# Decode attention with a parallel MLP: two weight rows to a partition, K0 loaded first, some w2 rows on the ACT queue, b1 spread by DVE

## Chip, cores, metric

One core of a Trainium2 chip. The time is the device time of one execution in microseconds (us), lower is better. The *span* is the stretch that the trace covers, from the first instruction to the last; the time is some 2 us longer. That remainder, time minus span, is called "outside the span" here. The runs record spans to 0.1 us, so a single value of it is good to 0.05 us.

Engines: PE is the matmul engine (PEld its weight loads), DVE, ACT and POOL are the vector, scalar and GpSimd engines, and SP issues most loads. The granted clock is the share of PE's full clock that the throttle allowed.

## The reference, cut to what matters

```python
x = A_x                                   # [2, 1, 576]
xn = layernorm(x)
# A: attention of one new token over the last 2048 cached positions (16 KV heads, 32 query heads, 128 wide)
q = xn @ wq                               # wq [576, 4096]
o = softmax(q @ K^T * 128**-0.5) @ V      # K and V are the bulk of the traffic
a = o @ wo                                # wo [4096, 576]
# B: MLP with squared ReLU
h = relu(xn @ w1 + b1) ** 2               # w1 [576, 4608]
b = h @ w2 + b2                           # w2 [4608, 576]
return x + a + b
```

Everything is bf16. K and V together are 33.6 MB of the 53.6 MB that have to be read once; the weights are the other 20 MB.

## The kernel before

It streams K and V in eight units of 2 MB each, and the weights between them. Nearly all loads are issued by SP. In names, K0 is K of the first unit; w2x and w2y are 240 and 16 rows of w2 that are loaded apart, in four loads and one, and `mlp_x` does their matmuls; "the remainder" is the last 64 of the 576 rows of wq or w1.

```python
NFULL = D // P                      # 4 full blocks of 128 rows, and a remainder of 64 rows
const = ctx.enter_context(tc.tile_pool(name="const", bufs=1))      # allocated first
kvpool = ctx.enter_context(tc.tile_pool(name="kvpool", bufs=6))    # K, V and w2 buffers, behind it
wbig = ctx.enter_context(tc.tile_pool(name="wbig", bufs=NFULL))
# ...
def issue_w(tiles, wt, c, name, width, lrem):          # wq and w1: one load per 128 rows
    if c < NFULL:
        tl = wbig.tile([P, WBW], BF16, tag="wbig", name=f"{name}_{c}")
        nc.sync.dma_start(out=tl[:, 0:width], in_=wt[c * P:(c + 1) * P, :])
# ...
def issue_w2x():                                       # 240 rows of w2, five partitions at a time
    ...
    nc.sync.dma_start(out=w2x_sb[i:XP:XP // XE, :], in_=rows[i])
# ...
x_sb = const.tile([B, D], BF16, name="x_sb")
nc.scalar.dma_start(out=x_sb[:], in_=x2d)
eps_t = const.tile([B, 1], F32, name="eps_t")
warm = const.tile([B, 2], F32, name="warm")            # 32 bytes to a partition as allocated
# ...
k0 = issue_kv(k_tiles, A_k_cache, 0, "k", parts=2)
issue_wq(0)
k0[0]()
issue_wq(1)
k0[1]()
for c in range(2, KC):
    issue_wq(c)
# ...
sel4 = const.tile([NG4, P], BF16, name="sel4")         # spreads b1 over the groups of the MLP
nc.gpsimd.memset(sel4[:], 0.0)
for b in range(B):
    nc.gpsimd.tensor_copy(out=sel4[:, b:P:32], in_=ident[0:NG4, 0:NG4])
# ...
mlp_h_end()
mlp_x()                                                # the matmuls of w2x and w2y
step(NU - 1, {}, with_pv=False)                        # transposes and scores of the last K
# ...
for i in range(len(W2P)):                              # w2, the last rows in pieces of 4, 2 and 1
    mlp_o(*W2P[i], last=(i == len(W2P) - 1))
nc.vector.tensor_copy(out=fin_sb[:], in_=out_ps[:])
nc.sync.dma_start(out=out2d[:, 0:OH], in_=fin_sb[0:B, :])
nc.scalar.dma_start(out=out2d[:, OH:D], in_=fin_sb[32:32 + B, :])
```

## Time and profile before

| | before |
|---|---|
| time, median of 3 runs | 137.41 us (137.2 to 137.5) |
| span of the profiled run | 135.0 us |
| first load packet starts, last load lands | 1.76 us, 131.27 us |
| output landed | 133.45 us |
| busiest engine, PE | 98.1 us, 73% |

The first lines of the page:

```profile
span 135.0 us, 4131 instructions
PE 98.1 (73%) x1876; PEld 79.8 (59%) x1876; DVE 56.8 (42%) x134; ACT 44.7 (33%) x51; POOL 10.2 (8%) x34
```

### The profile page before, as it was taken

The page shows a single profiled execution, that of the slowest core. Times are in us where ns is not written, and L with a number is a line of the kernel's source. Part 1 is how long each engine was busy: PE and PEld are TensorE (multiplying, and loading weights), DVE is VectorE, ACT ScalarE, POOL GpSimd, SP SyncE. Part 2 cuts the span into 40 slices and gives each one's busy share as a digit, 9 for nine tenths or more (in the row PEclk, how much of TensorE's full clock was granted, in tenths as well). Part 3 has the DMA queues.
Part 4 walks back from the last instruction along what each step waited for, and adds up shares of the span by engine and source line. Part 5 has one row for each costly group of instructions (what it writes and reads, how often), then busy time and mean ns, then how long its engine had stood idle before and what let it go on. Part 6 is the DMA issues. An engine that isn't in the chain of part 4 may idle for free.

```text
span 135.0 us, 4131 instructions
## 1 busy us (share of the span) xinstructions
PE 98.1 (73%) x1876; PEld 79.8 (59%) x1876; DVE 56.8 (42%) x134; ACT 44.7 (33%) x51; POOL 10.2 (8%) x34
## 2 busy tenths in 40 slices
PE   1039946699969179719997998796565999669961
PEld 0018616598859079607986997784115599655530
DVE  7532405574564634640455655644224024650001
ACT  6703504465254127110834625421021055010000
POOL 8300000110110110110001001001100000110000
PEclk9999995559999559955996899996555558965899
DMA  4999999999999999999999999999999999999950
GB/s 120 423 428 425 427 430 442 408 447 403 451 385 437 431 417 433 398 409 438 422 432 417 432 413 428 395 428 415 414 441 427 427 413 420 431 407 417 404 228 1
DMA packets 5492, 53.87 MB, mean 399 GB/s; under 512 B 694, under 2 KB 844, under 8 KB 1360
## 3 DMA queue, kind: packets, MB, share of 16 engines
q1 hardware_dynamic: 5404, 53.61, 95.1%
q8 instruction: 14, 0.23, 0.7%
q0 software_dynamic: 64, 0.01, 0.0%
q14 instruction: 2, 0.02, 0.0%
q10 hardware_dynamic: 8, 0.00, 0.0%
HBM read 53.62 MB, written 0.00 MB: 397 GB/s over the span
## 4 chain that ended last, share of the span: by engine, by line
DMA 87%; PE 6%; SPq 2%; DVE 1%; ACT 1%; issue 1%; ACTq 0%
DMA k<-in_A_k_cache_dram 39%; DMA w_rem<-in_B_w_dram 20%; DMA w<-in_B_w_dram 16%; DMA wq<-in_A_wq_dram 11%; PE out_ps L236 3%; PE kT_ps L271 2%; SPq L115 1%; SPq L109 1%; DVE hrow L376 1%; PE hb_ps L385 1%; ACT t L375 1%; PE ha_ps L382 1%; PE h_ps L366 0%; DVE fin_sb L502 0%; DVE hT_sb L391 0%
## 5 line engine op out<-in xcount | busy, mean ns | idle before, releaser
L271 PE MATMUL kT_ps<-ident,k 128*128 128x128 bf16 x512 | 44.9, 251 | 6.4 <-DMA k<-in_A_k_cache_dram 6.1
L274 ACT COPY kT<-kT_ps 128x1024 bf16<-128x1024 bf16 x32 | 32.1, 1011 | 36.0 <-PE kT_ps L271 34.4
L271 PEld LDWEIGHTS <-k 128*128 128x128 bf16 x512 | 37.2, 114 | 8.3 <-DMA k<-in_A_k_cache_dram 6.4
L276 DVE COPY kT<-kT_ps 128x1024 bf16<-128x1024 bf16 x32 | 21.8, 687 | 26.4 <-PE kT_ps L271 25.8
L286 PE MATMUL sc_ps<-qT_all,kT 128*128 128x8 bf16 x512 | 21.6, 168 | 4.5 <-ACT kT L274 2.6
L286 PEld LDWEIGHTS <-kT 128*128 128x128 bf16 x512 | 18.8, 99 | 6.3 <-ACT kT L274 3.5
L323 PE MATMUL oT_ps<-pT,v 128*128 128x8 bf16 x512 | 15.9, 166 | 2.0 <-ACT pT L303 1.5
L323 PEld LDWEIGHTS <-v 128*128 128x128 bf16 x512 | 14.4, 96 | 3.5 <-issue 3.4
L303 ACT ACTIVATE pT<-sub 128x512 bf16<-128x512 f32 x8 | 5.1, 631 | 26.0 <-DVE sub L300 26.0
L305 DVE TENSOR_REDUCE l<-pT 128x8 f32<-128x512 bf16 x8 | 8.5, 1065 | 5.3 <-ACT pT L303 5.3
L236 PE MATMUL out_ps<-wo,ws 128*2 128x288 bf16 x64 | 7.2, 403 | 3.5 <-DVE ws L345 3.5
L296 POOL PARTITION_ALL_REDUCE gmax<-m x8 | 2.9, 366 | 84.7 <-DVE m L294 84.7
L236 PEld LDWEIGHTS <-hT_sb 128*2 128x2 bf16 (+2 forms) x94 | 4.7, 96 | 5.4 <-issue 2.2
L292 DVE TENSOR_REDUCE m<-sc_ps 128x8 f32<-128x512 f32 x8 | 5.5, 692 | 4.7 <-PE sc_ps L286 4.6
L236 PEld LDWEIGHTS <-ws 128*2 128x2 bf16 x64 | 3.4, 110 | 6.0 <-DVE ws L345 3.6
L236 PE MATMUL out_ps<-w,hT_sb 128*2 128x288 bf16 x68 | 5.4, 302 | 1.4 <-DMA w<-in_B_w_dram 1.3
L366 PE MATMUL h_ps<-w,xnT 128*2 128x384 bf16 x48 | 4.3, 514 | 1.8 <-DMA w<-in_B_w_dram 1.7
L300 DVE TENSOR_TENSOR sub<-sc_ps,gm 128x512 f32<-128x512 f32 x8 | 5.5, 689 | 0.2
L307 POOL PARTITION_ALL_REDUCE lsum<-l x8 | 3.2, 400 | 23.7 <-DVE l L305 23.7
L502 DVE CAST fin_sb<-out_ps 34x288 bf16<-34x288 f32 x1 | 0.5, 451 | 10.3 <-PE out_ps L236 10.3
L366 PEld LDWEIGHTS <-xnT 128*2 128x2 bf16 x60 | 1.8, 104 | 5.1 <-issue 5.1
L236 PE MATMUL out_ps<-b_sb,ones_b 1*2 1x288 bf16 x2 | 0.4, 394 | 5.1 <-DMA b_sb<-in_B_b_dram 5.1
(73 smaller groups left out, 48.2 us busy)
## 6 DMA issues: line engine op xcount, KB each, us to landing
v<-in_A_v_cache_dram SPq DMA_DIRECT2D x8, 2048.0 KB, 23.8
k<-in_A_k_cache_dram SPq DMA_DIRECT2D x7, 2048.0 KB, 26.7
wo<-in_A_wo_dram SPq DMA_DIRECT2D x4, 1152.0 KB, 23.2
w<-in_B_w_dram SPq DMA_DIRECT2D x4, 1152.0 KB, 30.6
wq<-in_A_wq_dram SPq DMA_DIRECT2D x4, 1024.0 KB, 13.7
w<-in_B_w_dram SPq DMA_DIRECT2D x3, 1296.0 KB, 27.8
k<-in_A_k_cache_dram SPq DMA_DIRECT2D x2, 1024.0 KB, 7.4
w_rem<-in_B_w_dram SPq DMA_DIRECT2D x1, 576.0 KB
```

What stands on the lines that cost most here:

```text
L236: nc.tensor.matmul(out_ps[32 * i:32 * i + B, :], lhsT=lhsT, rhs=rhs_of(i * OH, (i + 1) * OH), start=start, stop=stop, skip_group_check=True)
L271: nc.tensor.transpose(out=kT_ps[:, i * P:(i + 1) * P], in_=k_sb[:, j * Dh:(j + 1) * Dh], identity=ident[:])
L274: nc.scalar.copy(out=kT[:], in_=kT_ps[:])
L276: nc.vector.tensor_copy(out=kT[:], in_=kT_ps[:])
L286: nc.tensor.matmul(sc_ps[:, g * JG + i, :], lhsT=kT[:, i * P:(i + 1) * P], rhs=qT_all[:, b, tq * NC:(tq + 1) * NC], start=True, stop=True)
L292: nc.vector.tensor_reduce(out=m1[:], in_=sc_ps[:].rearrange("p j c -> p c j"), axis=AX.X, op=ALU.max)
L300: nc.vector.tensor_tensor(out=sub[:], in0=sc_ps[:], in1=gm2[:].unsqueeze(1).to_broadcast([P, NJ, NC]), op=ALU.subtract)
L303: nc.scalar.activation(out=pT[:], in_=sub[:], func=ACT.Exp, scale=scale)
L305: nc.vector.tensor_reduce(out=l1[:], in_=pT[:].rearrange("p j c -> p c j"), axis=AX.X, op=ALU.add)
L307: nc.gpsimd.partition_all_reduce(lsum[:], l1[:], channels=P, reduce_op=ReduceOp.add)
L323: nc.tensor.matmul(oT_ps[:], lhsT=v_sb[:, j * Dh:(j + 1) * Dh], rhs=pT_tiles[u][:, j, :], start=(j == 0), stop=(j == NJ - 1))
L366: nc.tensor.matmul(mlp["ps"][k][32 * g:32 * g + B, :], lhsT=xnT[:, xc, :], rhs=rhs, start=False, stop=(c == KC - 1), skip_group_check=True ...
```

## The change

Its intent: fewer and longer pieces for wq and w1, a simpler start, a small load off the SP queue, and three small operations off POOL. The diff, cut to its core (index and naming lines left out):

```diff
-    wbig = ctx.enter_context(tc.tile_pool(name="wbig", bufs=NFULL))
+    RW = 2
+    wbig = ctx.enter_context(tc.tile_pool(name="wbig", bufs=NFULL // RW))
 ...
-            tl = wbig.tile([P, WBW], BF16, tag="wbig", name=f"{name}_{c}")
-            nc.sync.dma_start(out=tl[:, 0:width], in_=wt[c * P:(c + 1) * P, :])
+            tl = wbig.tile([P, RW * WBW], BF16, tag="wbig", name=f"{name}_{i}")
+            rows = wt[0:NFULL * P, :].rearrange("(p r) n -> p (r n)", r=NFULL)
+            nc.sync.dma_start(out=tl[:, 0:RW * width], in_=rows[:, i * RW * width:(i + 1) * RW * width])
+            for r in range(RW):
+                tiles[i * RW + r] = tl[:, r * width:(r + 1) * width]
 ...
+            if r0 == 0:      # the three last pieces of w2 share one tile
+                w2_last.append(wbig.tile([P, nr * D], BF16, tag="wbig", name=f"w2_{g}"))
+            tl = w2_last[0][:, r0 * D:r1 * D]
 ...
-            nc.sync.dma_start(out=w2x_sb[i:XP:XP // XE, :], in_=rows[i])
+            tc.keep_in_program_order(nc.scalar.dma_start(out=w2x_sb[i:XP:XP // XE, :], in_=rows[i]))
 ... (w2y likewise)
-    k0 = issue_kv(k_tiles, A_k_cache, 0, "k", parts=2)
-    issue_wq(0); k0[0](); issue_wq(1); k0[1](); then wq 2, 3 and the remainder
+    for f in issue_kv(k_tiles, A_k_cache, 0, "k"):
+        f()
+    for i in range(NFULL // RW + 1):
+        issue_wq(i)
 ... (x is transposed in the columns c, c+4, c+8, ... to match; K0 is transposed before all of q)
-    nc.gpsimd.memset(sel4[:], 0.0)
-    for b in range(B):
-        nc.gpsimd.tensor_copy(out=sel4[:, b:P:32], in_=ident[0:NG4, 0:NG4])
+    nc.vector.tensor_copy(out=sel4[:].rearrange("p (g s) -> p g s", s=32),
+                          in_=ident[0:NG4, 0:NG4].unsqueeze(2).to_broadcast([NG4, NG4, 32]))
 ...
     mlp_h_end()
-    mlp_x()
     step(NU - 1, {}, with_pv=False)
     ...
     wo_acc(NQ - 2)
+    mlp_x()
```

More of the change, by code (lines that the diff above doesn't have):

```diff
@@ L110, in issue_kv, with issue_w @@
                 for i in range(parts)]
-    def issue_w(tiles, wt, c, name, width, lrem):
-        if c < NFULL:
-            tl = wbig.tile([P, WBW], BF16, tag="wbig", name=f"{name}_{c}")
-            nc.sync.dma_start(out=tl[:, 0:width], in_=wt[c * P:(c + 1) * P, :])
+    def issue_w(tiles, wt, i, name, width, lrem):
+        if i < NFULL // RW:
+            tl = wbig.tile([P, RW * WBW], BF16, tag="wbig", name=f"{name}_{i}")
[3 more added lines that the diff above has]
+                tiles[i * RW + r] = tl[:, r * width:(r + 1) * width]
         else:
@@ L118, in issue_w @@
             nc.sync.dma_start(out=tl[:, 0:lrem], in_=wt[NFULL * P:D, :].rearrange("r (s l) -> (r s) l", s=S))
-        tiles[c] = tl
+            tiles[NFULL] = tl
     def issue_wq(c):
@@ L138, in issue_wo @@
         wo_tiles[tq] = tl
+    w2_last = []
     def issue_w2(g, r0, r1):
         nr = FR if g < NG4 - 1 else FT
-        pool, tag = (kvpool, "kv") if g < NG4 - 1 else (wbig, "wbig")
-        tl = pool.tile([P, (r1 - r0) * D], BF16, tag=tag, name=f"w2_{g}_{r0}")
+        if g < NG4 - 1:
+            tl = kvpool.tile([P, nr * D], BF16, tag="kv", name=f"w2_{g}")[:]
+        else:
+            if r0 == 0:
+                w2_last.append(wbig.tile([P, nr * D], BF16, tag="wbig", name=f"w2_{g}"))
+            tl = w2_last[0][:, r0 * D:r1 * D]
         rows = B_w2[g * HW:g * HW + nr * P, :].rearrange("(p r) n -> p (r n)", r=nr)
-        nc.sync.dma_start(out=tl[:], in_=rows[:, r0 * D:r1 * D])
+        nc.sync.dma_start(out=tl, in_=rows[:, r0 * D:r1 * D])
         w2_tiles[(g, r0)] = tl
@@ L155, in issue_w2x @@
             rows = B_w2[FX0:FX0 + XR * XP, :].rearrange("(e i r) n -> i e (r n)", e=XE, r=XR)
-            nc.sync.dma_start(out=w2x_sb[i:XP:XP // XE, :], in_=rows[i])
+            tc.keep_in_program_order(nc.scalar.dma_start(out=w2x_sb[i:XP:XP // XE, :], in_=rows[i]))
             if not x_parts:
-                nc.sync.dma_start(out=w2y_sb[:], in_=B_w2[FX0 + XR * XP:F, :])
+                tc.keep_in_program_order(nc.scalar.dma_start(out=w2y_sb[:], in_=B_w2[FX0 + XR * XP:F, :]))
     x_sb = const.tile([B, D], BF16, name="x_sb")
@@ L165 @@
     nc.scalar.activation(out=warm[:, 0:1], in_=eps_t[:], func=ACT.Sqrt)
-    k0 = issue_kv(k_tiles, A_k_cache, 0, "k", parts=2)
-    issue_wq(0)
-    k0[0]()
-    issue_wq(1)
-    k0[1]()
-    for c in range(2, KC):
-        issue_wq(c)
+    for f in issue_kv(k_tiles, A_k_cache, 0, "k"):
+        f()
+    NW = NFULL // RW + 1
+    for i in range(NW):
+        issue_wq(i)
     ones_f = const.tile([P, P], F32, name="ones_f")
@@ L208 @@
     for c in range(NFULL):
-        nc.tensor.transpose(out=pro_ps[:, c, :], in_=xn_sb[:, c * P:(c + 1) * P], identity=ident[:B, :B])
+        nc.tensor.transpose(out=pro_ps[:, c, :], in_=xn_sb[:, c:NFULL * P:NFULL], identity=ident[:B, :B])
     for sg in range(S):
@@ L436, in step @@
         softmax(u)
-    for g in range(4):
+    for g in range(NG):
         transposes(0, g)
-    q_block(0)
-    q_block(1)
-    for g in range(4, NG):
-        transposes(0, g)
-    for c in range(2, KC):
+    for c in range(KC):
         q_block(c)
@@ L470 @@
         if u == 4:
-            for c in range(KC):
-                issue_w1(c)
+            for i in range(NW):
+                issue_w1(i)
         if u + 3 < NU:
```

## The prediction

> **What bounds the kernel now.** I looked first at the slices of the page, to see which resource has no holes.
>
> ```profile
> DMA  4999999999999999999999999999999999999950
> GB/s 120 423 428 425 427 430 442 408 447 403 451 385 437 431 417 433 398 409 438 422 432 417 432 413 428 395 428 415 414 441 427 427 413 420 431 407 417 404 228 1
> DMA packets 5492, 53.87 MB, mean 399 GB/s; under 512 B 694, under 2 KB 844, under 8 KB 1360
> ```
>
> The DMA row stands at 9 from the second slice to the thirty-eighth, while the busiest engine, PE, is at 73% of the span. A 9 only means "at least 90%", so I asked for the busy time of each engine in stretches of the span, to see how full the engines are (columns: stretch, its length, busy us of PE, PEld, DVE, ACT, POOL, granted clock, DMA share, GB/s).
>
> ```profile
> 25.00:45.00 20.00, 16.76 (x384) 15.94 (x384) 11.62 (x24) 9.04 (x10) 1.84 (x5) 0.84 1.00 422
> 65.00:85.00 20.00, 18.02 (x429) 16.67 (x426) 11.82 (x25) 10.16 (x11) 1.53 (x4) 0.91 1.00 422
> 120.00:131.40 11.40, 9.34 (x121) 5.64 (x119) 0.84 (x4) 0.00 (x0) 0.32 (x1) 0.73 0.90 366
> ```
>
> The DMA share is 1.00 at 422 GB/s, and not even 18 us of PE work in 20 us lowers it. In the packet records the first load packet starts at 1.76 us and the last one lands at 131.27 us. These 129.5 us of stream, 1.76 us before it and 3.7 us after it make the span of 135.0 us; the measured time is 137.2 to 137.5, some 2.3 us more than the span.
>
> Next, the chain that ended last, to see whether anything else sets the end.
>
> ```profile
> DMA 87%; PE 6%; SPq 2%; DVE 1%; ACT 1%; issue 1%; ACTq 0%
> ...
> 109.30 22.09 DMA w<-in_B_w_dram
> 131.38 0.04 issue
> 131.42 0.68 PE out_ps L236 x6
> 132.10 0.02 issue
> 132.12 0.45 DVE fin_sb L502
> ```
>
> It is DMA but for the short calculations between, and it closes with the last w2 rows, six matmuls, one copy and the output. PE at the end says the same:
>
> ```profile
> 125.30 2.83 PE L236 MATMUL out_ps<-w,hT_sb 128*2 128x288 bf16 x36
> 129.24 1.27 PE L236 MATMUL out_ps<-w,hT_sb 128*2 128x288 bf16 x18 [1.12 <-DMA w<-in_B_w_dram]
> 130.66 1.42 PE L236 MATMUL out_ps<-w,hT_sb 128*2 128x288 bf16 x14 [0.16 <-DMA w<-in_B_w_dram]
> ```
>
> PE stood idle 1.12 us for the third w2 load and again for the pieces after it: it is ahead of the stream when the stream ends.
>
> Last, how the loads are issued, since the change moves five of them to ACT.
>
> ```profile
> 4.81 0.55 SPq L109 DMA_DIRECT2D k<-in_A_k_cache_dram  x1
> 5.53 0.54 SPq L109 DMA_DIRECT2D v<-in_A_v_cache_dram  x1
> 8.65 0.54 SPq L109 DMA_DIRECT2D k<-in_A_k_cache_dram  x1
> 10.96 0.54 SPq L109 DMA_DIRECT2D v<-in_A_v_cache_dram  x1
> 13.44 0.85 SPq L156 DMA_DIRECT2D w2x_sb<-in_B_w_dram  x1
> ...
> v<-in_A_v_cache_dram SPq DMA_DIRECT2D x8, 2048.0 KB, 23.8
> k<-in_A_k_cache_dram SPq DMA_DIRECT2D x7, 2048.0 KB, 26.7
> ```
>
> From 8.65 us on the issues come 2.4 us apart, the time of one 1 MB load, so each waits for a landing. The semaphores in the trace tell which: there are eight, handed out in turn to all loads of SP and ACT together (x_sb on ACT has the first, and the eighth load after it, K1, waits for that one). So a load waits for the eighth load before it. The last lines are the time from issue to landing: 23.8 and 26.7 us, of which a 2 MB load's own transfer is about 5 us at 422 GB/s. Some 18 to 22 us of work is therefore queued ahead of each load, and a delay of an issue costs nothing until it exceeds that.
>
> **What the Trainium skill says.** "DMA: Bandwidth & Descriptors", section "Specifications", gives a fabric ceiling of 435 GB/s for the 16 engines; the trace runs at 422, 97% of it, so only about 3% could be won by any shape of transfer. The same page, section "Why small descriptors are slow (HBM only)", has a fixed overhead of about three cycles for each packet. The trace agrees: its records give a median of 309 ns for a packet of 8,192 B and 614 ns for one of 16,384 B, so 2 x 309 - 614 = 4 ns is all that joining two of them saves. Section "Issuing engines are not separate DMA queues" says that starting DMAs from several engines saves only the sequencer's issue time; SP issues 42 loads at about 0.5 us, under 25 us in all, so that is not scarce here. Section "Why a DMA increments its semaphore by 16 and not by 1" says a load of 5 partitions runs on five engines only; each w2x load does have five packets of 13,824 B. The queue doesn't change that.
>
> **The change part by part.**
> Bytes: the same 53.6 MB.
> wq: 512 packets of 8,192 B become 256 of 16,384 B: 256 x 4 ns / 16 engines = 0.06 us. K0 in one load: 128 x 4 / 16 = 0.03 us. w1: 512 packets of 9,216 B (median 351 ns) become 256 of 18,432 B. From the 8,192 and 16,384 B packets the slope is 305 ns per 8,192 B with 4 ns fixed, which gives 690 ns for 18,432 B against 702 for two: 256 x 12 / 16 = 0.19 us. Five loads fewer (two of wq, two of w1, one of K0) save one 9 ns completion packet on each engine: 0.05 us. Together 0.3 us off the stream, all of it on the path.
> First packet: before, the first issue is a wq load of 0.40 us; K0 issues in 0.65 us. If the stream starts by that much later it costs up to 0.25 us; I take 0.1.
> w2x and w2y on ACT: five issues (4 x 0.75 + 0.43 = 3.4 us) leave SP, which spends most of its time waiting, and come to ACT, busy 44.7 of 135 us. Twenty packets of 518 ns on five engines remain 2.1 us on each of these five, whichever queue they come from. Nothing on the path.
> K0 first: q needs the remainder of wq, which lands last of these loads in both orders (19.1 us before), so the scores of unit 0 do not start earlier. PE does the 64 transposes of K0 in one go instead of in two. Nothing.
> b1 spread by DVE: takes a memset of 0.2 us and two copies of 0.19 us from POOL (10.2 us busy) and puts one small DVE copy, about 0.15 us, near the start. Nothing.
> mlp_x later: 26 matmuls, 3.26 us, leave the place before the transposes of the last K (104.4 us) for the tail. PE gains 3.26 us before and loses it after; with over 1.1 us of idle time for w2 and 2.2 us more for softmax between 117 and 121 us, it still waits for the last load. Nothing.
> wbig as two buffers of double width: the last w2 pieces wait for a pair of w1 blocks; both are calculated by 97 us, long before the last issue (114.2 us). Nothing.
> Sum: -0.3 + 0.1 = -0.2 us: 137.4 becomes 137.2.
>
> **Rivals.**
> (a) ACT stands in the ring of eight. An early w2x issue on ACT may have to wait there until a load eight before it lands, 7 to 19 us into the kernel, and behind it stand the LayerNorm square root and half of the K evacuations. For it: the semaphores show one ring for both engines, and ACT runs in order. Against a loss: it delays PE by at most some 10 us near the start, and 18 to 22 us of queued loads keep the stream full; PE needs 98 of 129 us and can catch up. If the buffers did run dry it would be 1 to 5 us: 138.5 to 142.
> (b) A new wait at the end: the three last w2 pieces share one tile now. If their matmuls waited for all three, 14 instead of 6 would follow the last landing: 8 x 0.1 = 0.8 us more, 138.2. Against: K0's halves share a tile before, and its transposes start at 10.58 us, ahead of the second half's landing (12.9 us).
> (c) Five engines end earlier or later. Engines drift apart by up to 3.3 us in mid-stream (completion times of one load), and at the end the 16 end some 1.5 us apart. If the new order evens this out it wins up to 0.7 us: 136.7. If it skews, as much is lost.
> (d) Pieces of 16 KB at a 32 KB pitch (wq) read HBM worse, or rows of 18,432 B better, than I reckon. No run shows it yet; 8.9 MB of 53.6 are concerned (21 us), so 5% either way is 1 us.
>
> **Range and chances.** The sum of certain terms is -0.2 us; (c) and (d) are symmetric at about 0.7 us, (a) and (b) only cost. Hence 136.4 to 138.3. Two per cent is 2.7 us. Faster by that much would need most of the 3% between 422 and 435 GB/s, which packets cannot give: 3%. Slower by that much needs (a) with a dry queue: 6%. The rest, 91%, is within 2%.
>
> **What would show it right or wrong.** DMA share 1.00 and 418 to 426 GB/s in the same stretches, 640 fewer data packets, the last load landing at 131.0 to 131.4 us, the same six matmuls after it. Rival (a) would show as a long ACT gap before 20 us, and only a DMA share under 0.97 somewhere would make it cost. Rival (b) would show 14 matmuls after the last landing. I am wrong if the time lies outside the range, or if the stretch between first and last packet differs from 129.2 us by more than 1 us.

## The result and the profile after

| | before | after |
|---|---|---|
| time, median of 4 runs | 137.45 us (137.20 to 137.64) | 136.46 us (136.43 to 136.55) |
| ratio, 95% interval | | 0.9930 [0.9913, 0.9947] |
| span, median | 135.2 us | 134.65 us |
| time outside the span, median | 2.13 to 2.21 us | 1.84 us |

Ratios here and below are the mean time of one kernel's fast runs over that of the other's of the same rounds, so not quite the ratio of the medians that are quoted. Executions over 1.5% slower than the fastest of the same kernel are left out of the means. The span of before is the median of the 11 runs that accompany each group of experiments. So the change is worth 0.95 to 1 us, within 2%: some 0.55 us of it in the span and 0.35 us outside.

The page of the changed kernel, first the engines and the stream:

```profile
span 134.7 us, 4124 instructions
PE 100.8 (75%) x1876; PEld 83.2 (62%) x1876; DVE 56.9 (42%) x135; ACT 44.3 (33%) x51; POOL 9.7 (7%) x31
...
GB/s 152 409 422 434 428 433 419 438 414 439 404 418 439 415 412 433 410 426 429 423 428 419 423 421 422 430 415 423 408 442 428 428 424 407 416 413 424 398 235 1
DMA packets 4772, 53.87 MB, mean 400 GB/s; under 512 B 614, under 2 KB 764, under 8 KB 1280
...
DMA 87%; PE 8%; SPq 2%; issue 0%; DVE 0%; ACT 0%; ACTq 0%
```

There are 720 fewer packets with the same bytes: the 640 data packets of the prediction and 80 completions. DMA is still 87% of the chain. The same stretches as before (stretch, length, busy us of PE, PEld, DVE, ACT, POOL, granted clock, DMA share, GB/s; the share can pass 1.00 because the records of packets overlap, at times 19 at once):

```profile
25.00:45.00 20.00, 17.34 (x344) 17.08 (x344) 9.60 (x19) 9.22 (x11) 1.53 (x4) 0.60 1.01 425
65.00:85.00 20.00, 17.41 (x408) 16.19 (x408) 11.83 (x25) 9.15 (x10) 1.53 (x4) 0.91 1.01 427
120.00:131.40 11.40, 10.34 (x112) 5.48 (x109) 0.00 (x0) 0.00 (x0) 0.00 (x0) 0.72 0.87 356
```

425 and 427 GB/s stand where 422 stood, but this is no general gain: in the other stretches between 8 and 120 us the rates are 428, 418, 424 and 417 where they were 430, 420, 424 and 418. Even a granted clock of 0.60 in the first stretch leaves the DMA share at 1.01. The chain that ended last runs through an ACT issue in its middle, and closes as before:

```profile
40.92 0.06 ACT kT L282
40.97 6.26 DMA w2x_sb<-in_B_w_dram
47.24 0.02 issue
47.25 0.02 SPq L110
47.27 0.03 issue
47.30 24.59 DMA k<-in_A_k_cache_dram
...
109.10 22.13 DMA w<-in_B_w_dram
131.23 0.04 issue
131.27 0.68 PE out_ps L244 x6
131.95 0.02 issue
131.97 0.45 DVE fin_sb L505
```

The last lines come 0.15 us earlier than before (131.27 for 131.42). PE at the end has the w2x matmuls in its tail now, and is still ahead of the stream:

```profile
120.30 3.04 PE L244 MATMUL out_ps<-w2x_sb,hT_sb 20*2 20x288 bf16 x24
...
129.11 2.83 PE L244 MATMUL out_ps<-w,hT_sb 128*2 128x288 bf16 x32 [0.81 <-DMA w<-in_B_w_dram]
```

The last number is the idle time before the group: PE waited 0.81 us for a w2 load. The three microseconds of w2x work in the tail were absorbed, and still six matmuls follow the last landing.

**What the stream itself won.** Packet records of the two traces: the mean busy time of an engine over all load packets fell from 128.35 to 127.72 us, 0.63 us. By size: the w1 pieces took 512 x 354.5 ns and take 256 x 694.5 ns (means, the first over all packets of 9,216 B, half of which are wo's), over 16 engines 0.23 us. The 768 packets of 8,192 B (mean 320.8 ns) gave way to 384 of 16,384 B; with all packets of 16,384 B together (1,920 x 618.6 before, 2,304 x 620.3 after) that is another 0.31 us. Completions and small differences are the other 0.09 us. Against it the first packet starts at 2.13 us instead of 1.76, 0.38 us later. Of this, 0.23 us is K0's longer issue (0.63 us, where wq's took 0.40); the rest has no record. The engines don't end together: the 16 completions of the last w2 load lie between 128.50 and 131.75 us before and between 128.14 and 131.60 after, and the last of them comes 1.00 and 1.17 us after their mean. The three add up, 0.38 - 0.63 + 0.17 = -0.08, about what the trace shows: the stream ends 0.14 us earlier in this pair (131.13 for 131.27).

**What comes after the stream.** The output lands 2.18 us after the last load in both. Then SP goes through the completion semaphores of its loads and stores. The instructions of the kernel's closing line, before and then after (queue and operation, count, ns shortest/median/longest, first and last start in us):

```profile
L530 SPq EVENT_SEMAPHORE  x8: 17/28/28, 132.9 to 134.9; - x8
...
L530 SPq DRAIN  x3: 7/7/13, 134.2 to 134.5; - x3
```

```profile
L533 SPq EVENT_SEMAPHORE  x8: 17/28/28, 132.8 to 134.6; - x8
...
L533 SPq DRAIN  x3: 7/7/13, 133.8 to 134.1; - x3
```

The first DRAIN marks the end of this walk: 0.72 us after the landing of the output before (133.45 to 134.17), 0.53 us after the change (133.30 to 133.83). What follows it is the same 0.84 and 0.83 us. The semaphore records show why. Loads and stores of SP and ACT take eight semaphores in turn, numbers 100, 102 and 113 to 118. Six waits of SP at the end go through 113 to 118 in this order, about 62 ns from one to the next. Before, there are 43 loads, and the two stores get 114 and 115: SP stands at them until the stores have landed, and 116, 117 and 118 come on top, 3 x 62 ns = 0.19 us. With 38 loads the stores get 117 and 118, and the other waits are over by then.

**Outside the span**, the runs (not the trace) show 0.35 us less. Which part of the change does it is a matter for the experiments.

### The profile page after: what moved, and what is told of

Read it like the earlier page. It is cut to its first block, busy times and chain, and to the rows that moved or that the text cites. A ratio compares the mean times of both kernels' runs of the same rounds, so it can differ in the third digit from the quotient of the medians.

```text
span 134.7 us, 4124 instructions
## 1 busy us (share of the span) xinstructions
PE 100.8 (75%) x1876; PEld 83.2 (62%) x1876; DVE 56.9 (42%) x135; ACT 44.3 (33%) x51; POOL 9.7 (7%) x31
## 4 chain that ended last, share of the span: by engine, by line
DMA 87%; PE 8%; SPq 2%; issue 0%; DVE 0%; ACT 0%; ACTq 0%
DMA v<-in_A_v_cache_dram 47%; DMA k<-in_A_k_cache_dram 18%; DMA w<-in_B_w_dram 16%; PE kT_ps L279 5%; DMA w2x_sb<-in_B_w_dram 5%; PE oT_ps L331 1%; PE sc_ps L294 1%; SPq L110 1%; SPq L117 1%; PE out_ps L244 1%; SPq L122 0%; DVE fin_sb L505 0%; ACT kT L282 0%; ACTq L282 0%
## 5 line engine op out<-in xcount | busy, mean ns | idle before, releaser
L279 PE MATMUL kT_ps<-ident,k 128*128 128x128 bf16 x512 | 49.5, 265 | 3.8 <-DMA k<-in_A_k_cache_dram 2.6
L279 PEld LDWEIGHTS <-k 128*128 128x128 bf16 x512 | 40.4, 121 | 5.3 <-DMA k<-in_A_k_cache_dram 2.8
L294 PEld LDWEIGHTS <-kT 128*128 128x128 bf16 x512 | 19.7, 101 | 7.0 <-ACT kT L282 3.4
L244 PE MATMUL out_ps<-wo,ws 128*2 128x288 bf16 x64 | 6.5, 363 | 0.0
L315 POOL PARTITION_ALL_REDUCE lsum<-l x8 | 3.2, 398 | 24.6 <-DVE l L313 24.6
L257 PE MATMUL q_ps<-wq,xnT 128*2 128x512 bf16 x32 | 3.3, 475 | 2.0 <-DMA wq<-in_A_wq_dram 2.0
```

What stands on the lines that cost most here:

```text
L244: nc.tensor.matmul(out_ps[32 * i:32 * i + B, :], lhsT=lhsT, rhs=rhs_of(i * OH, (i + 1) * OH), start=start, stop=stop, skip_group_check=True)
L257: nc.tensor.matmul(q_ps[k][32 * g:32 * g + B, :], lhsT=xnT[:, xc, :], rhs=rhs, start=(c == 0), stop=(c == KC - 1), skip_group_check=True, ...
L279: nc.tensor.transpose(out=kT_ps[:, i * P:(i + 1) * P], in_=k_sb[:, j * Dh:(j + 1) * Dh], identity=ident[:])
L294: nc.tensor.matmul(sc_ps[:, g * JG + i, :], lhsT=kT[:, i * P:(i + 1) * P], rhs=qT_all[:, b, tq * NC:(tq + 1) * NC], start=True, stop=True)
```

## The experiments

Twelve kernels in three groups; each group shares its runs of before (11, medians 137.25, 137.36 and 137.36 us). The first group ran on another chip than the other two, so kernels of different groups are best compared by their ratios to before. The diffs are cut to their core. The records name the theories by letters: in words, the later ones are the order of the first loads (D), the addresses of the tiles in SBUF (F), and the time outside the span as a matter of POOL's and SP's instruction streams (G). "Walk" is the stretch from the landing of the output to SP's first closing DRAIN in the profiled run.

### First group: one part of the change at a time

**e1_weights.** Before, with the double rows of wq and w1, K0 first and the shared w2 tile only.

```diff
+            nc.sync.dma_start(out=tl[:, 0:RW * width], in_=rows[:, i * RW * width:(i + 1) * RW * width])
+    for f in issue_kv(k_tiles, A_k_cache, 0, "k"): f()
+    for i in range(NFULL // RW + 1): issue_wq(i)
```

> The kernel before with only the weight and K0 part of the change (wq and w1 in two loads of two rows to a partition, K0 first in one load, one tile for the last w2 rows); w2x stays on SP, b1 spread on POOL, mlp_x early. Theory A (the gain of 1 us has three pieces: the last load lands 0.1 to 0.3 us earlier; the ring of eight is turned so that the two output stores hold its last two semaphores and SP's closing walk over the ring is 0.2 us shorter after the store lands; and an instruction fetch of 8,192 B that the kernel before makes 2 us after its span is gone, 0.4 us): five loads fewer put the stores on the last two semaphores too, so landing and walk gain here, 136.9 to 137.1; and 136.5 if the fetch is gone with SP at 69 instructions instead of 76. Rival B (the gain is in the stream: larger packets and a better order): 136.5 with the last landing 0.7 us or more earlier. Rival C (the ACT queue brings it): 137.4, no gain here.

Measured: 136.94 us, ratio 0.9958 [0.9936, 0.9980]; span 134.9, outside 2.07, walk 0.53 us, mean packet time 127.86 us. This part carries the shorter packets and the shorter walk (it has five loads fewer), so 0.3 us of the span.

**e2_actq.** Before, with w2x and w2y on ACT only (w2y's line, left out here, changes likewise).

```diff
-            nc.sync.dma_start(out=w2x_sb[i:XP:XP // XE, :], in_=rows[i])
+            tc.keep_in_program_order(nc.scalar.dma_start(out=w2x_sb[i:XP:XP // XE, :], in_=rows[i]))
```

> The kernel before with w2x and w2y on the ACT queue and nothing else. The number of loads stays 43, so the stores keep their place in the ring. Theory A: stream and walk as before, 137.3 to 137.5, or 137.0 if the fetch after the span goes with SP at 71 instead of 76 instructions. Rival B: 137.4. Rival C (ACT queue brings the gain): 136.5.

Measured: 137.28 us, ratio 0.9992 [0.9966, 1.0017]; span 135.2, outside 2.07, walk 0.72. By itself it does nothing to the span, and at most 0.06 us outside.

**e3_rest.** Before, with b1's spread on DVE and mlp_x later only.

```diff
-    nc.gpsimd.memset(sel4[:], 0.0)
-    for b in range(B):
-        nc.gpsimd.tensor_copy(out=sel4[:, b:P:32], in_=ident[0:NG4, 0:NG4])
+    nc.vector.tensor_copy(out=sel4[:].rearrange("p (g s) -> p g s", s=32), in_=...)
```

> The kernel before with only the DVE spread of b1 and mlp_x behind wo_acc. Theory A and rivals B and C: 137.4, nothing; PE does the last K's transposes 3 us earlier and still waits for the last w2 load. A gain of 0.4 us and no fetch after the span would say that the fetch belongs to POOL (62 to 59 instructions) and not to SP.

Measured: 137.31 us, ratio 0.9992 [0.9970, 1.0015]; span 135.15, outside 2.17. Nothing by itself. The medians of the three add up to 0.31 - 0.03 - 0.06 = 0.22 us, while the whole change won 0.95 to 1.0: something works only in company.

**e4_ring5.** After, with five small ACT loads behind the last activation, so that the stores take semaphores 114 and 115 again.

```diff
+    pad_sb = const.tile([B, 16 * 5], BF16, name="pad_sb")
+    for i in range(5):
+        tc.keep_in_program_order(nc.scalar.dma_start(out=pad_sb[:, 16 * i:16 * (i + 1)], in_=x2d[:, 16 * i:16 * (i + 1)]))
```

> The changed kernel with five loads of 32 B more on ACT behind its last activation, which turn the ring by five so that the stores hold the fourth and fifth semaphore as in the kernel before; SP's and POOL's instructions unchanged. Theory A: the last landing as in the changed kernel (131.1 us), the walk from the last store's landing to SP's last event 0.65 instead of 0.46 us, the time 0.2 us above the changed kernel (136.6 to 136.7), no fetch after the span. Rivals B and C: as the changed kernel, 136.5.

Measured: 136.35 us, ratio 0.9927 [0.9899, 0.9955], where 0.2 us more than after had been expected. A miss, although the walk is 0.73 us as foreseen. Five of six spans are 134.4 to 134.6 us, so something had won back what the walk lost. Two things were wrong with the experiment. The profiled run, the slowest, shows that the extra loads took part in the ring of eight: SP's last w2 loads waited for them, and the stream had a dip:

```profile
GB/s 151 388 434 427 431 431 431 431 416 437 416 411 441 397 426 436 406 446 412 436 412 431 416 433 418 432 430 428 401 429 441 412 431 409 416 337 401 414 225 1
```

The dip is the 337 in the thirty-sixth slice. And the new tile stands among the constants, ahead of the K, V and weight buffers, and moves all of them by 160 bytes. Packets of 10,368 B have a median of 389 ns here and 398 ns in after. That was the first sign that the address matters.

### Second group: the start, the ring, the addresses

**f1_remfirst.** After, with the remainder of wq ahead of K0.

```diff
+    issue_wq(NW - 1)
     for f in issue_kv(k_tiles, A_k_cache, 0, "k"):
         f()
```

> The changed kernel with the 0.5 MB remainder of wq issued first, then K0, then the rest of wq. Theory D (K0 first costs 0.38 us at the start: its issue takes 0.63 us and its first packets are 16 KB, so the first packet starts at 2.13 instead of 1.76 us): the stream starts at 1.75 to 1.85 us again, the last load lands 0.2 to 0.4 us earlier (130.8 us), the time falls to 136.1 to 136.3, below both kernels. Rival E (the first packets wait for memory anyway, what starts earlier only takes longer): as the changed kernel, 136.45.

Measured: 136.85 us over its four fast runs (137.62 over all six), ratio 0.9974 [0.9935, 1.0013]; two runs are slow ones. The first packet starts at 1.75 us, but the spans of the fast runs alone scatter between 134.5 and 136.3 us; the best run, 136.32 us, is 0.1 us under after's best. Starting earlier gained nothing that could be kept. Its profile fell in a slow run, so it explains nothing further, and why this order scatters stays open.

**f4_wqfirst.** After, with the first wq load ahead of K0: the stream starts early again, and nothing else differs.

```diff
+    issue_wq(0)
     for f in issue_kv(k_tiles, A_k_cache, 0, "k"):
         f()
```

> The changed kernel with the first two rows of wq before K0 instead of K0 first. If the 16 KB packets delay the start (theory D): first packet at 1.95 to 2.15 us, time as the changed kernel. If the form of K0's load does it: first packet at 1.8 us, last landing 0.2 to 0.3 us earlier, 136.1 to 136.3. If K0 first brought the gain: 136.6 or more.

Measured: 136.36 us, ratio 0.9935 [0.9921, 0.9949], span 134.6: the same as after (136.46, 134.65). The first packet starts at 1.75 us, and the mean packet time of an engine is 128.02 us, 0.30 us more than after's. So in this trace 0.38 us at the head came back as 0.30 us of longer packets, all in the first 4 us of the span; the completions of the last load have the same mean, 130.44 for 130.43. The profiled run is the slowest of the six (136.83 us), so the balance of a typical run is not shown. By the times, K0 first neither gains nor loses.

**f2_before_ring3.** Before, with three small ACT loads at the start, so that the stores take the last two semaphores; the tile lies among the constants.

```diff
+    pad_sb = const.tile([B, 16 * 3], BF16, name="pad_sb")
+    for i in range(3):
+        tc.keep_in_program_order(nc.scalar.dma_start(out=pad_sb[:, 16 * i:16 * (i + 1)], in_=x2d[:, 16 * i:16 * (i + 1)]))
```

> The kernel before with three loads of 64 B more on ACT behind x_sb at the very start, where they wait for nothing; they turn the ring by three, so that the stores hold the seventh and eighth semaphore as in the changed kernel. Theory A: from the landing of the last store to SP's closing drain 0.53 instead of 0.72 us, the span 135.0 instead of 135.2, time 137.05 to 137.15 against 137.25. Against theory A: 137.25 or more, walk 0.72.

Measured: 136.76 us, ratio 0.9956 [0.9944, 0.9968], span 134.6, walk 0.59 us. The time is below the range that was expected. The walk explains 0.13 us of the 0.6. The last load lands at 131.03 us and packets of 10,368 B take 389 ns: this experiment moves the buffers too, by 96 bytes, and can't settle the ring. Theory F was formed here.

**f3_after_sp8.** After, with eight small loads of SP behind the last w2 load, which lengthen SP's stream by eight instructions and move the buffers by 256 bytes, so to the same place within 256.

```diff
+    pad_sb = const.tile([B, 16 * 8], BF16, name="pad_sb")
+    for i in range(8):
+        tc.keep_in_program_order(nc.sync.dma_start(out=pad_sb[:, 16 * i:16 * (i + 1)], in_=x2d[:, 16 * i:16 * (i + 1)]))
```

> The changed kernel with eight loads of 64 B more on SP behind its last w2 load: SP has 72 instructions instead of 64, the ring is turned by eight, so not at all for SP's store. Theory A, in the form that the time outside the span depends on SP's length (measured: 1.82 us at 64, 2.07 at 69 and 71, 2.15 at 76): the span 134.6 to 134.9, the time outside it 2.05 to 2.1, so 136.7 to 136.9. If what lies outside the span has another cause (the combination of parts, POOL, ACT): outside 1.8, time 136.45.

Measured: 136.77 us, ratio 0.9955 [0.9942, 0.9968]; span 135.0, outside 1.82, walk 0.72 (ACT's store fell on semaphore 114). Eight SP instructions more cost nothing outside the span, so the time outside doesn't grow with SP's length. The 0.35 us in the span are 0.19 of the walk and something like 0.15 of the loads themselves.

### Third group: the ring without moved tiles, the time outside, the addresses alone

**g2_ring_clean.** As f2, but the tile comes from a pool that is allocated last, so that nothing moves.

```diff
+    padp = ctx.enter_context(tc.tile_pool(name="padp", bufs=1))
+    pad_sb = padp.tile([B, 16 * 3], BF16, name="pad_sb")
```

> The kernel before with three loads of 64 B more on ACT at the start into a tile that is allocated last, so that no other address moves. Theory A: the walk from the last store's landing to SP's closing drain 0.53 to 0.59 instead of 0.72 us, packets as before (398 ns at 10,368 B), the span 134.9 to 135.1 against 135.2, time 137.1 to 137.2 against 137.3. If the ring itself changes the stream: span 134.6.

Measured: 137.12 us, ratio 0.9982 [0.9969, 0.9995]; span 135.0 for 135.2 of before in the same rounds, outside 2.15 for 2.21. Packets of 10,368 B keep 396 ns. In its trace the first DRAIN starts at

```profile
L535 SPq DRAIN  x3: 7/7/13, 134.2 to 134.5; - x3
```

which is 0.60 us after its output landed (133.63), for 0.72 before. The walk is shorter by 0.12 us, and the ratio makes the time 0.25 us shorter, with an interval of 0.07 to 0.43. So the stores' place in the ring counts by itself.

**g3_pool.** After, with b1's spread back on POOL.

```diff
-    nc.vector.tensor_copy(out=sel4[:].rearrange("p (g s) -> p g s", s=32), in_=...)
+    nc.gpsimd.memset(sel4[:], 0.0)
+    for b in range(B):
+        nc.gpsimd.tensor_copy(out=sel4[:, b:P:32], in_=ident[0:NG4, 0:NG4])
```

> The changed kernel with the spread of b1 back on POOL (62 instead of 59 instructions on POOL, 64 on SP). Theory G (the time outside the span is the longer of two things, one of POOL and one of SP): span as the changed kernel (134.6), outside it 2.05 to 2.1 instead of 1.8, time 136.7. If POOL has nothing to do with it: outside 1.8, time 136.45.

Measured: 136.81 us, ratio 0.9956 [0.9942, 0.9970]; span 134.7 for 134.65, outside 2.06 (2.02 to 2.12) for 1.84. The three POOL operations cost 0.2 us outside the span (0.27 in the two profiled runs: 2.07 for 1.80) and next to nothing inside it. The times differ by 0.35 us; what is left of it is within the intervals of the two ratios.

**g4_actq_dve.** Before, with w2x on ACT and b1's spread on DVE together (e2 plus half of e3).

```diff
+            tc.keep_in_program_order(nc.scalar.dma_start(out=w2x_sb[i:XP:XP // XE, :], in_=rows[i]))
+    nc.vector.tensor_copy(out=sel4[:].rearrange("p (g s) -> p g s", s=32), in_=...)
```

> The kernel before with w2x and w2y on ACT and the spread of b1 on DVE, weights and K0 as before (59 instructions on POOL, 71 on SP, no fetch after the span). Theory G: span as the kernel before (135.2), outside it 1.8 instead of 2.15 us, time 136.95 to 137.05. If the outside part comes from the weights' loads: outside 2.06, time 137.25.

Measured: 136.92 us, ratio 0.9966 [0.9953, 0.9979]; span 135.1, outside 1.79 (1.77 to 1.84) for 2.21. Two parts that did nothing one by one win 0.4 us together. This is the table that the runs make, instructions of each engine counted in the traces, waits and issues included (the records count the program, in which SP has two more and POOL one):

| kernels | POOL | SP | outside the span, medians |
|---|---|---|---|
| before, g2, f2 | 61 | 74 | 2.13 to 2.22 us |
| e3 | 58 | 74 | 2.17 us |
| e1, e2, g3 | 61 | 62 to 69 | 2.06 to 2.07 us |
| after, g4, f3, f4, e4, g1 | 58 | 62 to 70 | 1.77 to 1.84 us |

It looks like the longest of three ends: one of about 2.15 us that goes with an SP stream of 74, one of 2.06 us with a POOL stream of 61, and 1.8 us of something else. Removing one leaves the next. For the first there is a record: before, e3, f2 and g2 have an instruction fetch of 8,192 B about 2 us after the end of the span (at 136.95 us before), and e1, e2, g4, f3 and after have none. For the second no trace has a record, so why three POOL operations cost 0.25 us there stays open. By this table the double rows alone bring SP under 74 (e1: 67), so the changed kernel would not need the ACT queue for it; no run combines e1 with b1's spread alone.

**g1_align.** After, with one tile 32 bytes wider. The instructions on all engines are the same; only the addresses behind it move, by 32 bytes. Addresses here and in the other experiments are those of the built programs; the traces don't show them. The K, V, w2, wq and w1 buffers start at multiples of 512 bytes in each partition instead of 32 bytes short of them.

```diff
-    warm = const.tile([B, 2], F32, name="warm")
+    warm = const.tile([B, 16], F32, name="warm")
```

> The changed kernel with one small constant tile 64 instead of 32 B wide, so that all tiles behind it, the K, V and weight tiles among them, start at a multiple of 64 B (of 512 B for the first) instead of 32 B past one; every engine's instructions are the same. Theory F (found in the fifth and seventh experiment's packets, where the added tile had moved the addresses in the same way: 389 instead of 398 ns for a packet of 10,368 B): packets of 10,368 B at 389 ns, of 16,384 B at 612 to 613, the span 134.2 to 134.4, time 136.05 to 136.2. If the address does nothing and those two runs were faster by their order of loads: packets at 398 ns, time 136.45.

Measured: 135.04 us (134.98 to 135.07, four runs), ratio 0.9828 [0.9813, 0.9843]; span 133.25, outside 1.77. It is the best kernel, 1.7% under before and 1.4 us under after, and far more than the 136.05 to 136.2 us that were expected. The page's first line and the same stretches of its trace:

```profile
span 133.3 us, 4124 instructions
```

```profile
25.00:45.00 20.00, 15.60 (x360) 15.00 (x360) 10.05 (x20) 10.34 (x11) 1.52 (x4) 0.83 1.01 429
65.00:85.00 20.00, 17.50 (x418) 16.35 (x418) 11.97 (x25) 9.15 (x10) 1.53 (x4) 0.91 1.01 430
```

The stream runs at 429 and 430 GB/s for after's 425 and 427, and at 426, 427 and 425 for 418, 424 and 417 in the other stretches from 45 to 120 us, with the same number of instructions and of load packets. Its last six matmuls start at

```profile
129.92 0.66 PE out_ps L244 x6
130.58 0.02 issue
130.60 0.45 DVE fin_sb L505
```

1.35 us before after's 131.27, and PE still waits for the last load:

```profile
127.82 2.74 PE L244 MATMUL out_ps<-w,hT_sb 128*2 128x288 bf16 x32 [0.27 <-DMA w<-in_B_w_dram]
```

The wait has shrunk from 0.81 to 0.27 us, but the stream still sets the end. Packet medians are 611 for 614 ns (16,384 B), 686 for 689 (18,432 B), 347 for 351 (9,216 B) and 389 for 398 (10,368 B); the mean of the 16,384 B ones is 616.4 for 620.3 ns, over 2,304 of them and 16 engines 0.56 us. All together an engine's packets take 126.66 us for 127.72, so 1.06 us of the 1.4. The 14 instruction fetches of 16,384 B, whose addresses did not move, shrink too, from 15.0 to 13.2 us in sum, which is 0.12 us on each of 16 engines; the rest has no record.

How far the address must be aligned can be read in part from four runs. Before's and after's buffers start at an odd multiple of 32 bytes. In f2 they start at a multiple of 64; f2 minus g2, the same ring without the move, is 136.76 - 137.12 = -0.36 us. In e4, built on after, they start at a multiple of 128, and it is as fast as after (ratios 0.9927 and 0.9930) although its walk is 0.2 us longer, so some -0.2 us. In g1, also built on after, it is a multiple of 512 (so also of 256), and -1.42 us. In f3 they moved by 256 and stayed at an odd multiple of 32: nothing was won. Whether 256 is enough no run separates. The Trainium skill, "DMA: Bandwidth & Descriptors", section "How a descriptor splits into AXI transactions", says that transfers are cut into transactions of 256 B that begin at multiples of 256, and that a descriptor which doesn't begin on one costs extra beats. The section gives this for reading. Here only the destination in SBUF moved, and packets became 3 to 9 ns shorter; that the cause is of the same kind is a guess.

## Why the prediction was right or wrong, point by point

**The bound: right.** DMA share 1.00 before, 1.01 after; PE was busy 2.7 us longer and it cost nothing; g1 then won 1.4 us with nothing but moved addresses, most of it in shorter packets. The stretch from first to last packet was 129.0 us where 129.2 were forecast. The forecast of 136.4 to 138.3 us held 136.46, but at its lower edge: the point, 137.2, was 0.75 us too high. That it held is luck. The room below the point had been given for evenly ending engines (c) and for kinder HBM reads (d); what filled it was SP's closing walk and the time outside the span, which the prediction had not counted.

**"Together 0.3 us off the stream": mis-sized, measured 0.63.** The term of w1 was right (0.19 predicted, 0.23 measured; the 690 ns for 18,432 B came out as 689). The term of wq and K0 was too small (0.09, measured 0.31). It used medians, 309 and 614 ns. But the first packets of the stream are slow: the first eight took 995 to 1,202 ns for 8,192 B before, some 0.8 us over the median, and the first sixteen 655 to 1,081 ns for 16,384 B after, at most 0.47 us over it. Summed over the first 4 us the excess is 0.46 us an engine before and 0.27 after, which is most of what the medians miss. How much of it recurs is not shown: in e1, with the same loads as after, it is 0.40 us.

**"First packet: I take 0.1": mis-sized, measured 0.38.** The two errors cancel: stream and head were to give -0.2 and give -0.25 us. f4 suggests that they are one thing: its stream started 0.38 us earlier than after's, and its packets took 0.30 us longer.

**"Five loads fewer ... 0.05 us": the step that missed the walk.** The completions are the size that was said. But fewer loads also move the two stores to the last semaphores of the walk, and SP's closing walk shrinks from 0.72 to 0.53 us. The prediction had found the ring of eight and used it only for the waits of loads; it took the 3.7 us after the stream as fixed, and measured they fell to 3.5. e1 has the same 0.53, e2 0.72, and g2 shortens the walk alone.

**"b1 spread by DVE: nothing" failed, and "w2x and w2y on ACT: nothing on the path" failed with it.** Inside the span both are right (e2, e3). Outside it they win 0.35 to 0.4 us, but only together (g4), and taking b1's part back costs 0.2 (g3). The prediction noted that the time is 2.3 us more than the span and never asked what of it the program decides.

**mlp_x later: nothing, right.** PE's longest wait for w2 went from 1.12 to 0.81 us, so it still waits.

**Rival (a)** was real as a coupling and cost nothing. The first two w2x issues on ACT went out without a wait, not as feared; a later one stood behind a K evacuation, and SP's K load waited for its slot. ACT's issues, and SP's wait (line, what it waited for, total us, times, longest):

```profile
4.43 1.53 ACTq L166 DMA_DIRECT2D w2x_sb<-in_B_w_dram  x2
...
26.86 0.68 ACTq L166 DMA_DIRECT2D w2x_sb<-in_B_w_dram  x1
...
40.97 0.68 ACTq L166 DMA_DIRECT2D w2x_sb<-in_B_w_dram  x1
```

```profile
SPq L110 <- DMA w2x_sb<-in_B_w_dram: 14.5, 3, 6.2
```

That load, at 47.30 us in the chain above, waited 6.2 us, and 24.6 us passed from there to its landing: the queue ahead of it swallowed the delay, as the prediction said it would up to 18 to 22 us. The DMA share is 1.01 from 25 to 45 us and 1.00 from 45 to 65. That it can bite shows in e4, where the same coupling near the end of the stream made the dip to 337 GB/s.

**Rival (b)** did not come: six matmuls after the last landing. (The half of K0 that speaks against it had landed by 13.42 us, not 12.9; the argument stands.) **(c)** gave nothing: the completions of the last load lie 3.25 us apart before and 3.46 after, and the last engine's lag on their mean went from 1.00 to 1.17 us. The 1.5 us that the prediction names for the end leaves out three engines that end earlier. **(d)** did not show: 18,432 B took 689 ns where 690 were reckoned, and the 256 packets of 16,384 B that follow K0's, in the time when wq loads, have a median of 611 ns.

**The sum.** Stream -0.15 to -0.35 us (by the pair of traces, and by the spans' medians less the walk), walk -0.19, outside -0.35: together -0.7 to -0.9 for -0.95 to -1.0 measured. From the parts, e1 (-0.31) and g4 (-0.44) make -0.75. The remaining 0.2 us lie in the span (134.65 against e1's 134.9) and no run explains them; it is about the scatter of e1's own spans. The later mlp_x is in neither e1 nor g4: e3 shows no gain from it, but no run takes it alone out of the changed kernel.

## What to carry to other kernels

When a kernel runs at the ceiling of its loads, count three things besides packets: the alignment of the load destinations in SBUF (here padding a small tile until the large buffers started on a multiple of 512 bytes cost nothing and won more than the whole change), what SP still walks through after the output has landed, and whether the time outside the span moves when a small operation leaves an engine. An experiment that adds a tile moves every address behind it, and one that adds a load moves every later load in the ring; allocate such a tile last, and check a size's packet median against the unchanged kernel before you believe the time. Where several ends lie close together outside or inside the span, taking the parts of a change one by one shows nothing for each, and only the pair shows the gain.

## What the Trainium skill lacked or had wrong

- "DMA: Bandwidth & Descriptors" gives the cost of an unaligned start for what a descriptor reads, and has nothing on what the start address of an SBUF destination costs. Here 32 bytes were worth 1.4 of 136.5 us (g1): 398 to 389 ns at 10,368 B, 614 to 611 ns at 16,384 B.
- The pages that were read say nothing of how loads and stores share eight completion semaphores and of the walk over them at the end: 0.72 against 0.53 us, about 62 ns a step.
- "Runtime: NRT & Kernel Launch", section "Instruction fetch mechanics", speaks of refills in blocks of 16 KiB. The traces show 14 of these, but also six to nine instruction fetches of 8,192 B; one of them, about 2 us after the span, goes with 2.15 us outside the span instead of 2.06. That POOL's stream of 61 instead of 58 instructions also costs some 0.25 us there is on no page that was read.
- That a stream can start 0.38 us earlier and gain nothing (f4: 136.36 for 136.46 us, packets 0.30 us longer in its one trace, that of its slowest run) is on no page that was read.
